# The last 64 keys' products with v as four 64 by 64 tiles, issued in front of the next scores

## The chip, the cores and the metric

One Trainium2 chip, one of its cores. The metric is the device time of one execution in microseconds (us), as the median of several runs. The engines are TensorE (PE, matmuls; PEld is its weight load), VectorE (DVE), ScalarE (ACT), GpSimd (POOL) and SyncE (SP, which issues DMAs).

## What is computed

```python
# q, k, v: (8 batches, 8 heads, 576 positions, 64), float32
scores = 1 / sqrt(64) * q @ k.T
scores = where(scores >= max(scores, -1) - tau, scores, -1e9)
attn   = exp(scores - max(scores, -1));  attn /= sum(attn, -1) + 1e-9
x      = heads side by side of (attn @ v)          # (8, 576, 512)
xn     = (x - mean) / sqrt(var + 1e-6) * g_ln      # over the 512 features
out    = x + max(xn @ w_ch1, 0) @ w_ch2            # 512 -> 2048 -> 512
```

## The kernel before, in words

**Slots.** A batch is worked off in nine slots (`SLOTS`), 72 in all (`NS`). Slots 0 to 3 take two heads each and their first 256 queries (`QH`), slot 4 (`s == HP`) takes the last 32 queries of each half for all heads, and slots 5 to 8 take the second 256 queries. In each slot the loop from L949 calls, in program order: the scores of this slot (L957), maxima, thresholds and exponentials (`exponentials`, L396), masks and sums (`weights`, L417), and the turning of the weights so that keys lie on partitions. Each engine works off its own instructions strictly in the order in which this loop issues them.

**Quarters.** A slot is cut into four quarters. `at_quarter(n, i, fn)` (L886) books a call for quarter `i` of slot `n`, and `run(n, i)` (L889) makes the booked calls; quarter -1 comes between the scores and the exponentials. Between them `second_part` (L900) puts in matmuls of the feed-forward part of an earlier group (a group is half a batch, 288 positions), as many as the planner's account of steps allows. So PE's queue is a chain of feed-forward matmuls (line L101, by the helper `product`, which splits a product into two column tiles of 64) into which scores and products with v are set.

**Scores.** `scores` (L373) multiplies the turned q by the turned k. The contraction is over 64 numbers, so it uses row tiles of 64: the two heads go to two PSUM tiles `sc[0]` and `sc[1]` of three banks each, in pieces of 384, 192, 320 and 256 columns (L390). In slot 4 these are four 64 by 64 tiles (`q_last`). The pieces lie at columns 128 to 1279 of each tile.

**Turned weights.** In batch 0, `turn_weights` (L452) turns the weights on PE by multiplying by a diagonal matrix, into tiles `tp` (512 keys, L461) and `tr` (the last 64 keys, L478), and ACT copies them to `em` and `er`. In later batches, `turn_blocks` (L493) turns 32 by 32 blocks on DVE, writes them to DRAM (`scr`), and `fetch` (L515), at quarter 0 of the next slot, reads them back: `em`, 512 keys as four chunks of 128, and `er`, the last 64 keys, on partitions 0 to 63 of one of two buffers `rests`, whose other 64 partitions are zero.

**Products with v.** `values_of` (L532) is booked for quarter 3 of the next slot (quarter 1 for the first five slots, `b == 0 and s <= HP`). For each of the two heads it multiplies the four chunks of v (`vt`) and then the last 64 keys (`vr`, from `v_rest`, partitions 64 to 127 zero) by 256 columns of weights (L550), all as 128 by 64 tiles. The result `pv` lies behind the scores in `sc[0]`, at columns 1280 to 1535 (`pv_behind`, L362), in the bank that holds the last scores too. In the first five slots it lies in a tile of its own. In slot 4 there are four pairs of heads of 64 columns each. After it ACT copies `pv` to `x` (L567, or L558 in slot 4), and POOL adds it to the sum over features (`add_feature`, L576).

**After the products.** `group_ready` (L925) books the mean of a group (`mean_of`, L585, a matmul that needs the sum), the centring (L599, DVE) and the feed-forward part two slots or so after its last product. `mean_of` puts itself off while the segments of the second feed-forward product hold both banks of PSUM. The relu of the first feed-forward product is ACT's (L729). Its PSUM tiles take turns between two banks.

**Loads.** `load_v` (L125) loads `vt` and `vr` for a pair of heads; POOL clears `rests` and `v_rest` once at the start (L151). SP issues these, the writes and reads of `scr`, the loads of q and k, and the stores. POOL scales q (L338) before DVE turns it (L345).

Of the kernel before, what the change touches and what calls it, by code (L numbers as in the profile page):

```python
# [8 lines left out]
F32 = mybir.dt.float32  # L9
# [9 lines left out]
def kernel(  # L19
# [31 lines left out]
    nc = tc.nc  # L51
    B, H, S, D = q.shape
# [41 lines left out]
    loaded, values_in, turned = {}, {}, {}  # L94
# [30 lines left out]
    def load_v(u):  # L125
        b, hp = units[u]
        vt = ins.tile([128, 2, J, D], F32, tag="v", name="v_in")
        vr = v_rest[hp]
        both = v[b, 2 * hp : 2 * hp + 2]
        if b:  # L130
            nc.sync.dma_start(
                out=vt.rearrange("p h c d -> p h (c d)"),
                in_=both[:, : J * 128].rearrange("h (p c) d -> p h (c d)", c=J),
            )
        for h in range(0 if b else 2):
            nc.sync.dma_start(
                out=vt[:, h], in_=both[h, : J * 128].rearrange("(c p) d -> p c d", p=128)
            )
# [257 lines left out]
    def exponentials(n):  # L396


        neg = small.tile([128, 4], F32, tag="neg", name="neg")
        thr = small.tile([128, 4], F32, tag="thr", name="thr")  # L400
        es = e_room[(n + 1) % 2 if n < SLOTS else 0]
        for h in range(2):
            i = slice(2 * h, 2 * h + 2)
            nc.vector.tensor_reduce(  # L404
                out=neg[:, i], in_=pairs[h],
                axis=AXL.X, op=ALU.max, negate=True,
            )
            nc.gpsimd.tensor_scalar(  # L408
                out=thr[:, i], in0=neg[:, i], scalar1=-1.0, scalar2=low_sb,
                op0=ALU.mult, op1=ALU.add,  # L410
            )
        for i in range(4):
            if i == 2:
                yield es, thr
            nc.scalar.activation(es[:, i], blocks[i], func=AF.Exp, bias=neg[:, i : i + 1])  # L415
# [31 lines left out]


    def turned_tiles(s):
        return att.tile([128, 4, J, 128], F32, tag="em", bufs=1, name="em"), rests[s % 2]  # L450

    def turn_weights(s, es, diags):  # L452


        em, er = turned_tiles(s)
        for i in range(4):
            if i:
                yield
            tp = ps_ff.tile([128, J, 128], F32, tag="ff", name="tp")
            for c in range(J):  # L460
                product(  # L461
                    tp[:, c], lhsT=es[:, i, c * 128 : (c + 1) * 128], rhs=diags[i],
                    start=True, stop=True,
                )
# [12 lines left out]
        for i in range(4):  # L477
            nc.tensor.matmul(  # L478
                tr[:, i], lhsT=es[:, i, J * 128 :], rhs=diags[i], start=True, stop=True
            )  # L480
        if s == HP:
            nc.scalar.copy(
                er[:64].rearrange("p a (u x) -> p u a x", u=HP),
                tr.rearrange("p u (a x) -> p u a x", a=4),
            )
        else:
            nc.scalar.copy(
                er[:64].rearrange("p a (h x) -> p h a x", h=2),
                tr.rearrange("p (h j) (a x) -> p h (j a) x", h=2, a=2),
            )  # L490
        yield em, er

# [34 lines left out]
    def x_of(g):  # L527
        if g not in groups:
            groups[g] = ffn.tile([128, NK, TOK], F32, tag="x", bufs=3, name="x")
        return groups[g]  # L530

    def values_of(b, s, turned_weights):  # L532

        em, er = turned_weights
        pv = pv_behind
        if b == 0 and s <= HP:
            pv = ps_ff.tile([128, QH], F32, tag="ff", name="pv")
        if s == HP:
            outs = [(hp, pv[:, hp * 64 : hp * 64 + 64]) for hp in range(HP)]
            pick = lambda t, hp, h: t[  # L540
                :, hp % 2 * 2 : hp % 2 * 2 + 2, (2 * h + hp // 2) * 32 : (2 * h + hp // 2) * 32 + 32
            ]
        else:
            outs = [(s if s < HP else s - HP - 1, pv)]
            pick = lambda t, hp, h: t[:, :, 64 * h : 64 * h + 64]
        for hp, dst in outs:
            vt, vr = values_in[b * HP + hp]
            for c in range(J + 1):
                for h in range(2):
                    nc.tensor.matmul(  # L550
                        dst[64 * h : 64 * h + 64],
                        lhsT=vt[:, h, c, :] if c < J else vr[:, h, :],
                        rhs=pick(em[:, :, c] if c < J else er, hp, h),
                        start=(c == 0), stop=(c == J),
                    )
        if s == HP:
            for t in range(2):
                nc.scalar.copy(  # L558
                    x_of(2 * b + t)[:, :, QH:],
                    pv.rearrange("p (u t x) -> p t u x", u=HP, t=2)[:, t],  # L560
                )
                for c in range(1, NK):
                    add_feature(2 * b + t, c, slice(QH, TOK))
        else:
            g = 2 * b + (s > HP)
            hp = outs[0][0]
            nc.scalar.copy(x_of(g)[:, hp, :QH], pv)  # L567
            if hp:
                add_feature(g, hp, slice(0, QH))
# [379 lines left out]
    for n in range(NS):  # L949
        b, s = divmod(n, SLOTS)  # L950
        ticks = (1, 3, 4)[: 2 + n // 3] if n < 6 else range(1, 7)

        def tick(i):
            if i in ticks:
                conversion.tick()

        scores(b, s)  # L957
        run(n, -1)
        rest = exponentials(n)
        es, thr = next(rest)  # L960
# [61 lines left out]
        drip({nc.vector: 2, nc.gpsimd: 0})  # L1022
    while later_calls or queue or aside or stores or drops:
        n += 1
        for i in range(QUARTERS):
# [35 lines left out]
```

## Time and profile before

| | |
|---|---|
| median of 3 runs | 1397.54 us (1396.71 to 1398.15) |
| the profiled execution | 1397.5 us, of which the span is 1395.7 us |
| PE busy | 1337.3 us, 96% of the span |
| DVE, POOL, ACT busy | 931.2, 609.7, 460.4 us |
| scores (L390), products with v (L550), busy | 150.6 and 130.8 us and smaller groups |
| granted clock of PE, mean | 0.993 |

The profile records one execution. The span is the time from its first instruction to its last; the rest of the execution's time lies around it. A float32 matmul leaves two records. A matmul's record is longer than the time for which it keeps the next one from starting, since they are pipelined; so what a group of matmuls costs is read from the starts of the groups behind it, not from the mean length of a record.

### The profile page before, as it was taken

The numbers are of one execution on the slowest core, as the hardware profiler recorded it, in microseconds if no ns is written. First come the engines' busy times: TensorE is split into PE (matmuls) and PEld (weight loads), VectorE is DVE, ScalarE is ACT, GpSimd is POOL, SyncE is SP. The second block draws the span as 40 slices with busy tenths as digits, with TensorE's granted clock in tenths as the row PEclk, the third lists the DMA queues.
The fourth block names the chain that finished last, engine by engine and source line by source line (L and its number), as shares of the span: only waits on it lengthen the run. The fifth ranks groups of instructions, "written<-read, shape, count | busy, mean of one in ns | idle before, by whom it ended". The sixth has DMA issues, their size and how long they took to land.

```text
span 1395.7 us, 35606 instructions
## 1 busy us (share of the span) xinstructions
PE 1337.3 (96%) x15048; PEld 986.9 (71%) x15048; DVE 931.2 (67%) x1638; ACT 460.4 (33%) x923; POOL 609.7 (44%) x809
## 2 busy tenths in 40 slices
PE   4888999999999999999999999999999999999996
PEld 3665665867768596877869586776858677685966
DVE  5998967676776767657776767657775767766211
ACT  3877613232332323232232323323232323323120
POOL 2444444544433454343444455353444444334413
PEclk8999999999999999999999999999999999999998
DMA  9722355447744476446754477445764476443211
GB/s 231 175 77 70 95 145 153 154 146 187 196 133 159 136 191 180 142 137 185 192 160 146 150 196 188 138 148 151 187 180 143 134 183 184 127 161 129 63 18 18
DMA packets 316383, 205.48 MB, mean 147 GB/s; under 512 B 242368, under 2 KB 273856, under 8 KB 308160
## 3 DMA queue, kind: packets, MB, share of 16 engines
q1 hardware_dynamic: 311456, 202.62, 50.8%
q8 instruction: 118, 1.93, 0.6%
q10 hardware_dynamic: 4736, 0.59, 0.4%
q14 instruction: 41, 0.34, 0.1%
q0 software_dynamic: 32, 0.00, 0.0%
HBM read 119.41 MB, written 83.76 MB: 146 GB/s over the span
## 4 chain that ended last, share of the span: by engine, by line
PE 89%; DVE 5%; ACT 2%; issue 1%; POOL 0%; POOLq 0%; DVEq 0%; ACTq 0%
PE p L101 36%; PE seg L101 30%; PE sc L550 10%; PE sc L390 10%; DVE e L422 1%; PE tp L101 1%; DVE neg L404 1%; PE var L101 0%; PE mean L101 0%; DVE w L269 0%; ACT e L415 0%; PE tr L478 0%; ACT part L812 0%; DVE hidden L296 0%; DVE w L296 0%
## 5 line engine op out<-in xcount | busy, mean ns | idle before, releaser
L101 PE MATMUL p<-xc,w 128*64 128x288 f32 x4096 | 518.1, 408 | 13.0 <-ACT hidden L729 5.5
L101 PEld LDWEIGHTS p<-xc,w 128*64 128x64 f32 x4096 | 288.9, 137 | 224.6 <-ACT hidden L729 16.0
L404 DVE TENSOR_REDUCE neg<-sc 128x2 f32<-128x1152 f32 x144 | 188.8, 1352 | 271.1 <-PE sc L390 271.0
L415 ACT ACTIVATE e<-sc,neg 128x576 f32<-128x576 f32 x288 | 196.8, 744 | 247.7 <-DVE neg L404 247.7
L438 POOL TENSOR_SCALAR e<-e,den 128x576 f32<-128x576 f32 x252 | 194.1, 783 | 134.5 <-DVE den L427 134.3
L101 PE MATMUL seg<-hidden,w 128*64 128x144 f32 x3840 | 248.0, 287 | 0.0
L101 PEld LDWEIGHTS seg<-hidden,w 128*64 128x64 f32 x3840 | 235.1, 137 | 11.6 <-issue 7.7
L422 DVE SCALAR_TENSOR_TENSOR e<-sc,thr,e 128x576 f32<-128x576 f32 x288 | 222.0, 810 | 13.9 <-ACT e L415 13.2
L729 ACT ACTIVATE hidden<-p 128x288 f32<-128x288 f32 x256 | 105.9, 414 | 241.0 <-PE p L101 239.2
L408 POOL TENSOR_SCALAR thr<-neg,low_sb 128x2 f32<-128x2 f32 x144 | 42.5, 295 | 306.1 <-DVE neg L404 302.1
L390 PE MATMUL sc<-kT,qT 64*128 64x384 f32 (+3 forms) x1024 | 150.6, 425 | 20.1 <-DVE qT L350 10.1
L504 DVE STREAM_TRANSPOSE et<-e 128x1152 f32<-128x1152 f32 x112 | 153.1, 1374 | 14.8 <-POOL e L438 14.0
L390 PEld LDWEIGHTS sc<-kT,qT 64*128 64x128 f32 x1024 | 94.3, 191 | 69.9 <-issue 18.2
L550 PE MATMUL sc<-em,v_in 128*64 128x256 f32 (+1 forms) x1408 | 130.8, 329 | 0.0
L101 PE MATMUL seg<-hidden,stage 128*64 128x144 f32 x1920 | 123.1, 286 | 0.0
L101 PEld LDWEIGHTS seg<-hidden,stage 128*64 128x64 f32 x1920 | 117.9, 137 | 3.5 <-issue 2.3
L550 PEld LDWEIGHTS sc<-em,v_in 128*64 128x64 f32 x1408 | 86.4, 137 | 32.2
L797 POOL TENSOR_TENSOR hidden<-hidden 128x576 f32<-128x576 f32 x60 | 84.4, 1426 | 27.3 <-ACT hidden L729 19.0
L576 POOL TENSOR_TENSOR sum<-sum,x 128x256 f32<-128x256 f32 (+1 forms) x64 | 32.6, 509 | 113.2 <-ACT x L567 110.7
L797 DVE TENSOR_TENSOR hidden<-hidden 128x576 f32<-128x576 f32 x60 | 49.1, 853 | 47.8 <-PE seg L101 38.1
L567 ACT COPY x<-sc 128x256 f32<-128x256 f32 x60 | 22.3, 372 | 164.7 <-PE sc L550 115.3
L812 ACT COPY part<-seg 128x288 f32<-128x288 f32 x75 | 30.1, 401 | 131.2 <-PE seg L101 109.6
(151 smaller groups left out, 1186.6 us busy)
## 6 DMA issues: line engine op xcount, KB each, us to landing
scr<-et SPq DMA_DIRECT2D x63, 1152.0 KB, 4.9
em<-scr SPq DMA_DIRECT2D x63, 1024.0 KB, 5.9
out_dram<-ot SPq DMA_DIRECT2D x256, 36.0 KB, 4.9
q_in<-in_q_dram SPq DMA_DIRECT2D x124, 72.0 KB, 2.7
k_in<-in_k_dram SPq DMA_DIRECT2D x120, 72.0 KB, 3.0
rest<-scr SPq DMA_DIRECT2D x63, 128.0 KB, 6.0
v_in<-in_v_dram SPq DMA_DIRECT2D x28, 256.0 KB, 5.2
w<-in_moe_w_ch_dram SPq DMA_DIRECT2D x10, 512.0 KB, 6.2
```

The lines of the kernel that those rows point to most:

```text
L101: nc.tensor.matmul(out[r], lhsT=lhsT[:, r], rhs=rhs, **flags)
L390: nc.tensor.matmul(sc[h][64 * i : 64 * i + 64 if s == HP else 128, at : at + n], lhsT=ql[r] if s == HP else qT[r, half, j * 128 : (j + 1) ...
L404: nc.vector.tensor_reduce(out=neg[:, i], in_=pairs[h], axis=AXL.X, op=ALU.max, negate=True,)
L408: nc.gpsimd.tensor_scalar(out=thr[:, i], in0=neg[:, i], scalar1=-1.0, scalar2=low_sb, op0=ALU.mult, op1=ALU.add,)
L415: nc.scalar.activation(es[:, i], blocks[i], func=AF.Exp, bias=neg[:, i : i + 1])
L422: nc.vector.scalar_tensor_tensor(out=es[:, i], in0=blocks[i], scalar=thr[:, i : i + 1], in1=es[:, i], op0=ALU.is_ge, op1=ALU.mult, accum_o ...
L438: nc.gpsimd.tensor_scalar(out=es[:, i], in0=es[:, i], scalar1=den[:, i : i + 1], scalar2=1.0, op0=ALU.mult, op1=ALU.mult,)
L504: nc.vector.transpose(et[:, :, 64 * h : 64 * h + 64].rearrange("p n (j c) -> p j n c", j=2), es[:, 2 * h : 2 * h + 2].rearrange("p j (n c) ...
L550: nc.tensor.matmul(dst[64 * h : 64 * h + 64], lhsT=vt[:, h, c, :] if c < J else vr[:, h, :], rhs=pick(em[:, :, c] if c < J else er, hp, h) ...
L576: nc.gpsimd.tensor_tensor(out=sums[g][:, cols], in0=x[:, 0, cols] if c == 1 else sums[g][:, cols], in1=x[:, c, cols], op=ALU.add,)
L729: nc.scalar.activation(hidden[:, d], p1, func=AF.Relu)
L797: eng.tensor_tensor(out=out[at], in0=in0[at], in1=in1[at], op=op)
```

## The change

The products of the 512 keys are cut in two halves of 128 columns (`j`), of which one goes to the columns behind `sc[0]` and one to those behind `sc[1]`. They stay at quarter 3. The last 64 keys are laid out twice as high: `er` has the queries of half 0 on partitions 0 to 63 and those of half 1 on 64 to 127, in one buffer, and `v_rest` holds v's last 64 rows on both halves of the partitions, loaded twice. Their products are four tiles of 64 rows by 64 columns, two heads by two halves of the queries, issued at a new point, quarter -3, just in front of the scores of the slot after next. ACT's copy of half 1 comes at quarter -2, just behind these scores; its copy of half 0 comes at a point "copy" in `exponentials`, behind the maxima and thresholds and in front of the first exponential. POOL's sums come at quarter 0 of that slot. For the first five slots all of it stays in place, with a rest on 128 rows (the other half is zero). The turned leftover `tr` of batch 0 is written to two column tiles instead of one.

```diff
-    rests = [consts.tile([128, 4, 128], F32, name=f"rest{i}") for i in range(2)]
-    v_rest = [consts.tile([128, 2, D], F32, name=f"v_rest{i}") for i in range(HP)]
+    er_sb = consts.tile([128, 2, 128], F32, name="er")
+    v_rest = [consts.tile([128, 2, 2, D], F32, name=f"v_rest{i}") for i in range(HP)]
...
-        nc.sync.dma_start(out=vr[:64], in_=both[:, J * 128 :].rearrange("h p d -> p h d"))
+        for j in range(2):
+            nc.sync.dma_start(
+                out=vr[64 * j : 64 * j + 64, j], in_=both[:, J * 128 :].rearrange("h p d -> p h d")
+            )
...
-    for t in rests + v_rest:
+    for t in v_rest:
         nc.gpsimd.memset(t, 0.0)
...
-    pv_behind = sc[0][:, FREE + 2 * S : FREE + 2 * S + QH]
+    pv_behind = [t[:, FREE + 2 * S : FREE + 2 * S + 128] for t in sc]
...
+        run(n, "copy")
         for i in range(4):
             if i == 2:
                 yield es, thr
...
-        tr = ps_ff.tile([64, 4, 128], F32, tag="ff", name="tr")
+        tr = ps_ff.tile([128, 2, 128], F32, tag="ff", name="tr")
         for i in range(4):
-            nc.tensor.matmul(
-                tr[:, i], lhsT=es[:, i, J * 128 :], rhs=diags[i], start=True, stop=True
-            )
+            rest = es[:, i, J * 128 :]
+            if s == HP:
+                to = tr.rearrange("p a (b x) -> p (a b) x", b=2)[:, i]
+                for half in range(2):
+                    at = slice(64 * half, 64 * half + 64)
+                    nc.tensor.matmul(to[at], lhsT=rest, rhs=diags[i][:, at], start=True, stop=True)
+            else:
+                h, j = divmod(i, 2)
+                nc.tensor.matmul(
+                    tr[64 * j : 64 * j + 64, h], lhsT=rest, rhs=diags[i], start=True, stop=True
+                )
...
-        nc.sync.dma_start(out=er[:64], in_=scr[:, J * 128 :].rearrange("a p x -> p a x"))
+        for j in range(2):
+            nc.sync.dma_start(
+                out=er[64 * j : 64 * j + 64],
+                in_=scr[2 * j : 2 * j + 2, J * 128 :].rearrange("a p x -> p a x"),
+            )
...
+        for c in range(J):
+            for (hp, j, dst, pick), first in zip(outs, firsts):
+                vt, _ = values_in[b * HP + hp]
                 for h in range(2):
                     nc.tensor.matmul(
-                        dst[64 * h : 64 * h + 64],
-                        lhsT=vt[:, h, c, :] if c < J else vr[:, h, :],
-                        rhs=pick(em[:, :, c] if c < J else er, hp, h),
-                        start=(c == 0), stop=(c == J),
+                        dst[64 * h : 64 * h + 64], lhsT=vt[:, h, c, :],
+                        rhs=pick(em[:, 2 * j : 2 * j + 2, c], h), start=c == 0 and first, stop=False,
                     )
+        def rest():
+            for (hp, j, dst, pick), last in zip(outs, lasts):
+                _, vr = values_in[b * HP + hp]
+                rows = slice(0, 128) if at_once else slice(64 * j, 64 * j + 64)
+                for h in range(2):
+                    nc.tensor.matmul(
+                        dst[64 * h : 64 * h + 64], lhsT=vr[rows, j, h],
+                        rhs=pick(er[rows], h), start=False, stop=last,
+                    )
...
+        if at_once:
+            rest()
+            copy(0)
+            copy(1)
+            add()
         else:
+            n = b * SLOTS + s + 2
+            at_quarter(n, -3, rest)
+            at_quarter(n, -2, copy, 1)
+            at_quarter(n, "copy", copy, 0)
+            at_quarter(n, 0, add)
...
+        run(n, -3)
         scores(b, s)
+        run(n, -2)
         run(n, -1)
```

More of the change, by code (lines that the diff above doesn't have):

```diff
@@ L449, in turned_tiles @@
     def turned_tiles(s):
-        return att.tile([128, 4, J, 128], F32, tag="em", bufs=1, name="em"), rests[s % 2]
+        return att.tile([128, 4, J, 128], F32, tag="em", bufs=1, name="em"), er_sb
     def turn_weights(s, es, diags):
@@ L475, in turn_weights @@
                 )
-        tr = ps_ff.tile([64, 4, 128], F32, tag="ff", name="tr")
+        tr = ps_ff.tile([128, 2, 128], F32, tag="ff", name="tr")
         for i in range(4):
-            nc.tensor.matmul(
-                tr[:, i], lhsT=es[:, i, J * 128 :], rhs=diags[i], start=True, stop=True
-            )
+            rest = es[:, i, J * 128 :]
[9 more added lines that the diff above has]
+                )
         if s == HP:
             nc.scalar.copy(
-                er[:64].rearrange("p a (u x) -> p u a x", u=HP),
-                tr.rearrange("p u (a x) -> p u a x", a=4),
+                er.rearrange("p a (u x) -> p u a x", u=HP),
+                tr.rearrange("p v (w a x) -> p (v w) a x", w=2, a=2),
             )
@@ L487, in turn_weights @@
             nc.scalar.copy(
-                er[:64].rearrange("p a (h x) -> p h a x", h=2),
-                tr.rearrange("p (h j) (a x) -> p h (j a) x", h=2, a=2),
+                er.rearrange("p a (h x) -> p h a x", h=2),
+                tr.rearrange("p h (a x) -> p h a x", a=2),
             )
@@ L534, in values_of @@
         em, er = turned_weights
+        at_once = b == 0 and s <= HP
         pv = pv_behind
-        if b == 0 and s <= HP:
-            pv = ps_ff.tile([128, QH], F32, tag="ff", name="pv")
+        if at_once:
+            both = ps_ff.tile([128, 2, 128], F32, tag="ff", name="pv")
+            pv = [both[:, j] for j in range(2)]
         if s == HP:
-            outs = [(hp, pv[:, hp * 64 : hp * 64 + 64]) for hp in range(HP)]
-            pick = lambda t, hp, h: t[
-                :, hp % 2 * 2 : hp % 2 * 2 + 2, (2 * h + hp // 2) * 32 : (2 * h + hp // 2) * 32 + 32
-            ]
-        else:
-            outs = [(s if s < HP else s - HP - 1, pv)]
-            pick = lambda t, hp, h: t[:, :, 64 * h : 64 * h + 64]
@@ L546, in values_of @@
-        for hp, dst in outs:
-            vt, vr = values_in[b * HP + hp]
-            for c in range(J + 1):
+            outs = [
+                (hp, hp % 2, pv[hp % 2][:, hp // 2 * 64 : hp // 2 * 64 + 64],
+                 lambda t, h, hp=hp: t[:, :, (2 * h + hp // 2) * 32 : (2 * h + hp // 2) * 32 + 32])
+                for hp in range(HP)
+            ]
+        else:
+            outs = [
+                (s % (HP + 1), j, pv[j], lambda t, h: t[:, :, 64 * h : 64 * h + 64])
+                for j in range(2)
+            ]
@@ L549, in values_of @@
+        banks = [0 if at_once else j for _, j, _, _ in outs]
+        firsts = [banks.index(bank) == i for i, bank in enumerate(banks)]
+        lasts = [bank not in banks[i + 1 :] for i, bank in enumerate(banks)]
+        for c in range(J):
+            for (hp, j, dst, pick), first in zip(outs, firsts):
+                vt, _ = values_in[b * HP + hp]
                 for h in range(2):
                     nc.tensor.matmul(
-                        dst[64 * h : 64 * h + 64],
-                        lhsT=vt[:, h, c, :] if c < J else vr[:, h, :],
@@ L553, in values_of @@
-                        rhs=pick(em[:, :, c] if c < J else er, hp, h),
-                        start=(c == 0), stop=(c == J),
-                    )
-        if s == HP:
-            for t in range(2):
+                        dst[64 * h : 64 * h + 64], lhsT=vt[:, h, c, :],
+                        rhs=pick(em[:, 2 * j : 2 * j + 2, c], h), start=c == 0 and first, stop=False,
+                    )
+        def rest():
[7 more added lines that the diff above has]
+                    )
@@ L558, in values_of, with copy @@
+        def copy(j):
+            if s == HP:
+                for t in range(2):
+                    nc.scalar.copy(
+                        x_of(2 * b + t)[:, :, QH:].rearrange("p (a j) x -> p j a x", j=2)[:, j],
+                        pv[j].rearrange("p (a t x) -> p t a x", a=2, t=2)[:, t],
+                    )
+            else:
                 nc.scalar.copy(
-                    x_of(2 * b + t)[:, :, QH:],
-                    pv.rearrange("p (u t x) -> p t u x", u=HP, t=2)[:, t],
-                )
@@ L562, in values_of, with add @@
-                for c in range(1, NK):
-                    add_feature(2 * b + t, c, slice(QH, TOK))
-        else:
[L565 to L569, printed above, removed]
+                    x_of(2 * b + (s > HP))[:, s % (HP + 1), 128 * j : 128 * j + 128], pv[j]
+                )
+        def add():
+            if s == HP:
+                for t in range(2):
+                    for c in range(1, NK):
+                        add_feature(2 * b + t, c, slice(QH, TOK))
+            elif s % (HP + 1):
+                add_feature(2 * b + (s > HP), s % (HP + 1), slice(0, QH))
@@ L571, in add_feature @@
+        if at_once:
+            rest()
+            copy(0)
+            copy(1)
+            add()
+        else:
+            n = b * SLOTS + s + 2
[3 more added lines that the diff above has]
+            at_quarter(n, 0, add)
     def add_feature(g, c, cols):
@@ L1024 @@
         n += 1
+        for i in (-3, -2, -1, "copy"):
+            run(n, i)
         for i in range(QUARTERS):
```

## The prediction, made before the change was run

> **What bounds the kernel now.** I read the page's busy times and its chain first.
>
> ```profile
> PE 1337.3 (96%) x15048; PEld 986.9 (71%) x15048; DVE 931.2 (67%) x1638; ACT 460.4 (33%) x923; POOL 609.7 (44%) x809
> ...
> PE 89%; DVE 5%; ACT 2%; issue 1%; POOL 0%; POOLq 0%; DVEq 0%; ACTq 0%
> ```
>
> TensorE (PE) holds the end: 89% of the chain. The table of stretches agrees: from 240 to 1310 us PE is busy 1065.6 of 1070. So there, what PE no longer streams is gained in full, and what it newly waits for is lost in full. Before 240 us, DVE and ACT take turns on the chain, and each item has to be looked up there.
>
> Next the PE timeline of one slot in the middle. Columns: start, length, operation, records. Two matmuls side by side leave four records, so two records are one pass of a pair. Lengths overlap, so I use differences of starts.
>
> ```profile
> 613.16 1.90 PE L550 MATMUL sc<-em,v_in 128*64 128x256 f32 x16
> 614.89 0.60 PE L550 MATMUL sc<-rest,v_rest 128*64 128x256 f32 x4
> 615.32 2.60 PE L101 MATMUL p<-xc,w 128*64 128x288 f32 x20
> 617.85 2.21 PE L390 MATMUL sc<-kT,qT 64*128 64x384 f32 x16
> 619.99 6.04 PE L101 MATMUL p<-xc,w 128*64 128x288 f32 x48
> 625.86 0.66 PE L101 MATMUL var<-hidden,avg_sb 128*64 128x288 f32 x4
> ```
>
> The last 64 keys (rest) cost 615.32 - 614.89 = 0.43 us: two passes of 256 columns, 0.216 each, 0.84 ns a column. A pass of 288 columns takes 0.243. The ten passes from 615.32 should end at 617.75, but the scores start at 617.85: 0.10 late. The scores stream 2 x 1152 columns, 1.94 us, and hold PE 2.14: 0.20 more. The 24 passes after them take 5.87, not 5.82: 0.05 more. So a visit to the 64-row, 128-column shape costs 0.35 us beyond its columns. The same reading for the scores of the last queries, which run as 64 by 64 tiles:
>
> ```profile
> 243.20 1.62 PE L101 MATMUL p<-xc,w 128*64 128x288 f32 x12
> 244.75 2.17 PE L390 MATMUL sc<-kT,q_last 64*64 64x384 f32 x32
> 246.85 2.16 PE L101 MATMUL p<-xc,w 128*64 128x288 f32 x16
> 248.84 0.91 PE L101 MATMUL seg<-hidden,w 128*64 128x144 f32 x12
> ```
>
> 0.10 before, 2.10 - 1.94 = 0.16 inside, 0.05 after: 0.31. And 32 records in the time of 16 say that four 64 by 64 tiles do run together, at the column rate of two.
>
> [...]
>
> **Part by part, steady state.** 67 slots' products use the deferred path (63 of batches 1 to 7, and four of batch 0).
> - Rest: four tiles of 128 columns together, 2 passes x 0.109 = 0.22, for 0.43: -0.21.
> - em products: 8 passes of 256 become 16 of 128. Transposes of 128 columns (tp) take 3.58 us for 32 passes, entry included, so a pass costs 0.109 to 0.112 and loads don't bind. 16 x 0.109 = 1.75 for 1.73: +0.02 (0.00 to 0.07).
> - One more change of shape per slot: [...] +0.16. No row shows 64 by 64 going to 64 by 128. [...] Dearer than any seen is possible; I allow +0.06.
>
> Of the 67, 51 are followed by wide scores: -0.03 each, -1.5 us. Seven stand before the 64 by 64 scores, so no change is added: -0.19 each, -1.3. Seven are the last-query products: their 40 passes with em take 2.33 us (273.56 to 275.89), 0.058 each; rest goes from 8 passes to 4, -0.23 + 0.16 = -0.07 each, -0.5. The last two have no scores behind them and pay a whole visit: +0.12 each, +0.2. Sum -3.1 us.
>
> **Batch 0.** Here the weights are turned on PE, and the leftover (tr) goes from one column tile to two.
>
> ```profile
> 122.28 3.75 PE L101 MATMUL tp<-diag,e 128*64 128x128 f32 x64
> 125.86 1.07 PE L478 MATMUL tr<-diag,e 128*64 128x128 f32 x8
> 126.72 2.15 PE L101 MATMUL p<-xc,w 128*64 128x288 f32 x16
> ```
>
> Eight records in 0.86 us, one tile at a time; paired, 0.43. Four of nine (97, 126, 148, 180 us) lie on PE's part of the chain: -1.7. The one at 32 us lies on the chain with its ACT copy (0.58 for 512 elements per partition; 256 take 0.37): -0.6. The other four are covered by DVE, whose pieces fill the chain from 36 to 89 us: nothing. SyncE issues each rest of v twice (0.7 to 1.9 us each at the start) ahead of the weight fetches. First use of a weight chunk is at 18.2 us, with issue at 10.9 and 5.5 to land: nothing taken, up to +1.5. In the first five slots the rest stays on 128 rows, 4 passes of 128 for 2 of 256: nothing. POOL's first memsets differ by less than 1 us and end near 2.3 us; its next work waits for q until 8.8: nothing.
>
> **What moves.** The copies go to the head of the next slot.
>
> ```profile
> 620.16 2.62 DVE L404 TENSOR_REDUCE neg<-sc 128x2 f32<-128x1152 f32 x2 [7.55 <-PE sc L390]
> 621.61 1.37 ACT L415 ACTIVATE e<-sc,neg 128x576 f32<-128x576 f32 x2 [3.23 <-DVE neg L404]
> 622.87 0.41 ACT L729 ACTIVATE hidden<-p 128x288 f32<-128x288 f32 x1
> ```
>
> Copy 1 waits for the scores and runs under the first maximum (1.35 us). The second maximum waits for it: hidden. Copy 0 waits for the first maximum and delays both exponentials and the relu behind them. A copy of 256 takes 0.37, of 288 0.40: 128 about 0.26, less overlap, so 0.2 to 0.3 late. PE needs that relu's bank at 619.99 + 0.05 + 16 x 0.243 = 623.93; it is free at 623.28: 0.65 in hand. The last-query slot copies in four pieces, perhaps 0.4 late: still covered. DVE's masks come 0.3 later; the next scores are 8 us behind them.
>
> POOL's sums move behind the thresholds. For even groups six adds (1.74 us at 596.7) then end about 4.9 us after the scores; the mean on PE comes 5.7 after: covered by 0.8. Where the head also scales q, the sum stands ahead of that. This costs only where the chain goes through it, once:
>
> ```profile
> 195.27 0.06 POOL thr L408
> 195.34 0.18 issue
> 195.52 0.75 POOL q_in L338
> 196.28 0.02 issue
> 196.30 0.04 DVE qT L345
> ```
>
> One add of 0.74 goes in front of q_in: +0.74 at the next start of PE (201.73), which now waits 1.86 there for DVE. The early mean at 194.85 will wait some 1.4 inside that same time. At 232.96 the exponentials are on the chain: copy 0 adds 0.2. Sum +0.9. On SyncE one more DMA per slot (leftover in two halves) sits behind em's at the slot's head, needed a slot later; with one buffer instead of two it waits for the rest products, which stand before the scores, while its issue comes 1.2 us after their start (635.90 to 634.67): nothing.
>
> **Sum.** -3.1 - 2.3 + 0.9 = -4.5 us. The profiled execution took 1397.5 us (span 1395.7 and 1.8 around it), like the median of 1397.54: 1393.0.
>
> **Rivals.** (1) [...] 0.21 less on 58 slots, -12 us more, 1381. [...] (2) The change is dearer than any seen, or four tiles that accumulate lose a little: 0.06 to 0.09 over 58 slots takes back 3.5 to 5 us: 1396.5 to 1398, no difference. (3) Slower: relus at the slots' heads. Two heads in each of 14 groups have 0.65 us in hand. If copy 0 (its wait, its time, its handover) comes to 0.95 us instead of 0.3, PE stands 0.3 at each of 28 heads, +8: 1401. It decides from 0.65 on. For it: the copy is in front of everything ACT does then. Against it: the waits show no such stall today,
>
> ```profile
> PE p L101 <- ACT hidden L729: 5.5, 3, 2.8
> ```
>
> three times in all, at the start, and no copy of this size nears 0.65.
>
> **Numbers.** The forecast case has 0.64, spread 1389.5 to 1396.5 by the switch's bounds; 0.10 of it lies within 0.2% (2.8 us, about what a measurement of this kernel can tell from no change). Rival 1: 0.11, faster. Rival 2: 0.14, of it 0.02 slower. Rival 3: 0.11, of it 0.01 within. Faster 0.65, same 0.23, slower 0.12. From 1387 to 1399 leaves out most of rivals 1 and 3.
>
> **What would show it.** In the timeline after: rest as 8 records in about 0.22 plus 0.05, a first score 0.22 late, em in 1.75, p to rest 0.10. tr in 0.43. No new row "PE p <- ACT hidden" in the middle; PE's mean at 195 waiting for POOL. Wrong, if rest to scores shows no gap (rival 1) or over 0.3 (rival 2), or if p waits for ACT in every group (rival 3).

## The result, and the profile after

The changed kernel takes 1399.23 us, median of 4 runs (1396.44 to 1400.06), against 1397.57 for the kernel before in the same comparison: a ratio of 1.0009 with a 95% interval from 0.9991 to 1.0026. No difference can be told. The forecast was 1393.0, faster; the result lies 6.2 above it, at the upper edge of the range that was given (1387 to 1399). The profiled execution took 1399.81 us, span 1398.0.

The page's busy times and its chain, for the changed kernel:

```profile
PE 1332.8 (95%) x16336; PEld 1011.1 (72%) x16336; DVE 928.2 (66%) x1638; ACT 464.2 (33%) x1003; POOL 607.1 (43%) x807
...
PE 83%; DVE 7%; ACT 2%; DMA 2%; issue 2%; POOL 1%; SPq 1%; POOLq 0%; DVEq 0%; ACTq 0%
```

PE is 4.5 us less busy, and yet the end is no earlier: PE's share of the chain fell from 89% to 83%, DVE's rose from 5% to 7%, and POOL now has a share. From 240 to 1310 us PE is busy 1061.9 of 1070, where it was 1065.6. So the work became shorter and PE waits more. First the work: PE's timeline of the middle slot that the prediction read, in the changed kernel (start, length, operation, records).

```profile
614.81 1.92 PE L574 MATMUL sc<-em,v_in 128*64 128x128 f32 x32
616.56 2.60 PE L101 MATMUL p<-xc,w 128*64 128x288 f32 x20
619.08 0.45 PE L584 MATMUL sc<-er,v_rest 64*64 64x128 f32 x8
619.46 2.21 PE L393 MATMUL sc<-kT,qT 64*128 64x384 f32 x16
621.60 6.04 PE L101 MATMUL p<-xc,w 128*64 128x288 f32 x48
```

The products with em take 616.56 - 614.81 = 1.75, as worked out. Ten passes of p end at 616.56 + 2.43 = 618.99 and the rest starts at 619.08: 0.09 for the change of shape. From the rest to the scores 0.38; if the columns take 0.22 of it, as worked out from passes of 128, 0.16 is the second change. The scores hold PE 2.14, as before. In front of the 64 by 64 scores the same rest takes less:

```profile
246.02 0.45 PE L584 MATMUL sc<-er,v_rest 64*64 64x128 f32 x8
246.29 2.12 PE L393 MATMUL sc<-kT,q_last 64*64 64x384 f32 x32
```

0.27 instead of 0.38, for no change of shape lies between. All this is as forecast. Now the waits of PE, from the table of waits (engine, line, tile, releaser: us in total, times, longest):

```profile
PE p L101 <- ACT hidden L779: 5.5, 3, 2.7
...
PE seg L101 <- DVE hidden L847: 3.8, 6, 0.6
...
PE mean L101 <- POOL sum L626: 1.2, 1, 1.2
```

The first line, rival 3's, is what it was before (5.5, three times). The second is new: six times 0.63, once in each of batches 2 to 7, between the scores of their slots 1 and 2. The third is new too, and foreseen.

How one of the six comes about is seen in the timelines of the same place (a bracket gives the idle time ahead of an instruction and what ended it). The kernel before:

```profile
833.67 8.23 PE L101 MATMUL seg<-hidden,w 128*64 128x144 f32 x128
...
835.05 0.27 POOL L408 TENSOR_SCALAR thr<-neg,low_sb 128x2 f32<-128x2 f32 x1 [0.99 <-DVE neg L404]
835.30 0.74 POOL L338 TENSOR_SCALAR q_in<-q_in,scl_sb 128x576 f32<-128x576 f32 x1
...
836.00 0.81 POOL L816 TENSOR_TENSOR y<-y 128x288 f32<-128x288 f32 x1
836.07 0.77 DVE L345 STREAM_TRANSPOSE qT<-q_in 128x256 f32<-128x256 f32 x2 [0.45 <-POOL q_in L338]
...
836.89 1.38 POOL L816 TENSOR_TENSOR y<-y,part 128x288 f32<-128x288 f32 x1
836.90 1.99 DVE L797 TENSOR_TENSOR hidden<-hidden 128x576 f32<-128x576 f32 x2
```

PE's segments stand in one group, without a wait in the table. The changed kernel:

```profile
835.32 4.09 PE L101 MATMUL seg<-hidden,w 128*64 128x144 f32 x64
...
836.63 0.27 POOL L411 TENSOR_SCALAR thr<-neg,low_sb 128x2 f32<-128x2 f32 x1 [0.99 <-DVE neg L407]
...
836.86 0.73 POOL L626 TENSOR_TENSOR sum<-sum,x 128x256 f32<-128x256 f32 x1
...
837.58 0.75 POOL L341 TENSOR_SCALAR q_in<-q_in,scl_sb 128x576 f32<-128x576 f32 x1
...
838.36 0.77 DVE L348 STREAM_TRANSPOSE qT<-q_in 128x256 f32<-128x256 f32 x2 [1.15 <-POOL q_in L341]
...
839.18 2.00 DVE L847 TENSOR_TENSOR hidden<-hidden 128x576 f32<-128x576 f32 x2
...
840.04 2.18 PE L101 MATMUL seg<-hidden,w 128*64 128x144 f32 x32 [0.63 <-DVE hidden L847]
```

The sum stands between the second threshold and q_in. DVE's turn of q waits for it 0.70 longer, and what is queued behind that turn on DVE has nothing to do with q: the operand difference for PE's next segments (L847). Before, it started 836.90 - 833.67 = 3.23 us behind the segments; here it starts 839.18 - 835.32 = 3.86 behind, and PE waits 0.63. Even before it came without slack: in a run further down, where it starts 3.16 behind, the 128 records that take 8.23 here take 8.16.

### The profile page after: what moved, and what is told of

The parts are those of the page before. It is cut to its first block, busy times and chain, and to the rows that moved or that the text cites. A ratio compares the mean times of both kernels' runs of the same rounds, so it can differ in the third digit from the quotient of the medians.

```text
span 1398.0 us, 38357 instructions
## 1 busy us (share of the span) xinstructions
PE 1332.8 (95%) x16336; PEld 1011.1 (72%) x16336; DVE 928.2 (66%) x1638; ACT 464.2 (33%) x1003; POOL 607.1 (43%) x807
## 4 chain that ended last, share of the span: by engine, by line
PE 83%; DVE 7%; ACT 2%; DMA 2%; issue 2%; POOL 1%; SPq 1%; POOLq 0%; DVEq 0%; ACTq 0%
PE p L101 34%; PE seg L101 27%; PE sc L393 10%; PE sc L574 8%; PE sc L584 2%; DVE e L426 2%; DVE neg L407 1%; DMA v_in<-in_v_dram 1%; SPq L116 1%; PE tp L101 1%; DMA et<-in_moe_w_ch_dram 1%; POOL q_in L341 1%; PE var L101 0%; PE mean L101 0%; POOL sum L626 0%
## 5 line engine op out<-in xcount | busy, mean ns | idle before, releaser
L574 PE MATMUL sc<-em,v_in 128*64 128x128 f32 (+1 forms) x2368 | 129.5, 263 | 0.0
L574 PEld LDWEIGHTS sc<-em,v_in 128*64 128x64 f32 x2368 | 122.9, 137 | 7.8
L597 ACT COPY x<-sc 128x128 f32<-128x128 f32 x120 | 31.8, 266 | 260.7 <-PE sc L393 193.5
L847 POOL TENSOR_TENSOR hidden<-hidden 128x576 f32<-128x576 f32 x60 | 84.8, 1429 | 47.8 <-ACT hidden L779 38.2
L847 DVE TENSOR_TENSOR hidden<-hidden 128x576 f32<-128x576 f32 x60 | 49.2, 854 | 49.1 <-PE seg L101 39.1
L101 PE MATMUL seg<-hidden,e 128*64 128x144 f32 x960 | 65.3, 286 | 0.0
```

The source lines that it names most:

```text
L101: nc.tensor.matmul(out[r], lhsT=lhsT[:, r], rhs=rhs, **flags)
L574: nc.tensor.matmul(dst[64 * h : 64 * h + 64], lhsT=vt[:, h, c, :], rhs=pick(em[:, 2 * j : 2 * j + 2, c], h), start=c == 0 and first, stop= ...
L597: nc.scalar.copy(x_of(2 * b + (s > HP))[:, s % (HP + 1), 128 * j : 128 * j + 128], pv[j])
L847: eng.tensor_tensor(out=out[at], in0=in0[at], in1=in1[at], op=op)
```

## The experiments

Most alter one thing, in the changed kernel or in the one before; two put two edits together. To see where in the run a difference arises, I list when PE starts the scores of a slot, as the offset to the kernel before in the profiled executions (us; "end" is PE's last matmul). "Sum at head" is the kernel before with the sums moved; "behind q" and "behind adds" are the changed kernel with the sums later, "and mean" the latter with a later mean; "v upper" is the kernel before with the added loads.

```
slot   changed  sum at head  behind q  behind adds  and mean  v upper
  2     -1.78      -1.26       -0.78      -0.97      -1.25     -0.22
  4      1.60      -1.33       -1.39       2.63      -0.02     -0.21
  7      0.78       0.36       -0.57       1.86      -1.08     -0.18
  9      0.74       0.38       -0.63       1.83      -2.25      0.38
 11      1.70       1.77        0.80       1.89      -3.64      0.39
 18      1.28       1.71        0.37       1.48      -1.41      0.40
 71      2.12       5.93       -0.03      -1.87      -4.52      0.43
end      2.35       5.93        0.20      -1.63      -4.28      0.43
```

Up to slot 7 single executions differ by up to 4 us (in slot 4 by -1.39 to 2.63 among four kernels whose program is the same there). So the place of a loss is read from slot 7 on, and the start from medians only. In part this is the granted clock of PE. It was 0.50 from 18.5 to 28.5 us in the kernel before, and from 49.5 to 52.5 and from 77 to 80 us in the changed one. Between slots 6 and 7, ten passes that take 2.65 us in both of these, at a clock of 1.00, take 4.22 in "behind q"; the offset there rises by 1.6.

**The sums alone.** The kernel before, with nothing altered but the place of POOL's sums: at the head of a later slot, as in the changed kernel.

```diff
...
-            if hp:
-                add_feature(g, hp, slice(0, QH))
+            add = lambda: hp and add_feature(g, hp, slice(0, QH))
+        if b == 0 and s <= HP:
+            add()
+        else:
+            at_quarter(b * SLOTS + s + 2, 0, add)
```

> The kernel before with only POOL's sums moved, to quarter 0 of the next slot, in front of the scaling of q. Theory A (this move alone makes the stalls): six or seven waits of PE seg for DVE hidden of about 0.6 us, and 0.4 and 0.6 at slots 9 and 10: +4.5 to +5, 1402 to 1402.6. Rival B (it takes the late exponentials as well): fewer waits, 1398 to 1399.5.

Measured: 1402.70 us against 1397.58, ratio 1.0038 (1.0024 to 1.0052). Its table of waits:

```profile
PE seg L101 <- DVE hidden L802: 4.2, 6, 0.7
PE mean L101 <- POOL sum L581: 1.3, 1, 1.3
```

Six times 0.70, and 1.39 between slots 9 and 11 in the offsets. This one move costs 5.1 us and makes both waits, without any of the changes on PE. Turned round: the change without it should beat the kernel before by some 3 to 4 us.

**The sums behind q.** The changed kernel, with the sum behind the scaling of q instead of ahead of it.

```diff
-            at_quarter(n, 0, add)
+            at_quarter(n, "sum", add)
...
                 load_qk(u + 1)
+        run(n, "sum")
         if n < SLOTS + HP:
...
```

> The changed kernel with POOL's sums over features issued behind the scaling of q instead of in front of it. Theory A (the sum in front of q's scaling makes DVE late; once per batch PE then waits 0.63 us for the operand difference that DVE has behind its transposes, and slots 9 and 10 lose about 0.4 and 0.6): the six waits of PE seg for DVE hidden vanish, -3.8 us, and about -0.4 to -0.9 at slots 9 and 10 (the early mean still waits for the sum): 1394 to 1396. Rival B (the stall comes from the copies on ACT or from DVE's second maximum waiting for a copy): the six waits stay, 1399.

Measured: 1398.69 us (1397.12 to 1402.28) against 1397.28, ratio 1.0013 (1.0007 to 1.0020). That can't be told apart from the changed kernel, and is not what I expected. By the offsets, slots 18 to 71 fall by 0.40, where the changed kernel's rise by 0.84. The waits say why:

```profile
PE seg L101 <- DVE hidden L847: 2.5, 6, 0.4
PE mean L101 <- POOL sum L626: 1.9, 1, 1.9
```

The stall has shrunk to 0.41 and is not gone. The same place in this kernel's timeline:

```profile
836.05 0.73 POOL L626 TENSOR_TENSOR sum<-sum,x 128x256 f32<-128x256 f32 x1
836.12 0.77 DVE L348 STREAM_TRANSPOSE qT<-q_in 128x256 f32<-128x256 f32 x2 [0.44 <-POOL q_in L341]
836.74 0.80 POOL L866 TENSOR_TENSOR y<-y 128x288 f32<-128x288 f32 x1
...
836.94 2.48 DVE L847 TENSOR_TENSOR hidden<-hidden 128x576 f32<-128x576 f32 x2
...
838.30 4.14 PE L101 MATMUL seg<-hidden,w 128*64 128x144 f32 x64 [0.41 <-DVE hidden L847]
```

DVE turns q in time again (0.44 of idle). But the sum has pushed POOL's add of y to 836.74, just ahead of DVE's difference. Of the difference's two instructions the first takes 1.21 instead of 0.72 and ends at 838.15, 0.61 after the add has ended (836.74 + 0.80 = 837.54). The add starts 0.20 ahead, and of the 0.60 us that the two stand side by side, DVE loses 0.49. In the kernel before this add ends at 836.81, ahead of the difference at 836.90. A second add starts there 0.01 ahead of the difference (836.89), and it is that add which is longer (1.38; another of its kind takes 0.79 at 599.35). What decides which of the two takes longer is not shown.

**The sums behind the adds.** So the sum goes later still, ahead of POOL's scaling of the weights, where it stands idle for 2.4 us. In the last-query slot and slot 10, where a mean needs the sum at once, it stays at the head.

```diff
-            at_quarter(n, 0, add)
+            at_quarter(n, 0 if s == HP or n == 10 else "sum", add)
...
         tick(2)
+        run(n, "sum")
         blocks_go = by_blocks(b * HP)
...
```

> The changed kernel with POOL's sums put still later in the slot: behind the scaling of q and behind the adds of y, just ahead of POOL's scaling of the weights, where POOL stands idle for 2.4 us. The two kinds of slot whose mean on TensorE needs the sum at once (the last-query slot and slot 10) keep it at the head. Theory A: the trace of the run with the sum directly behind q shows q on time (0.44 us of idle ahead of qT, as before the change), but now the sum delays POOL's adds of y by 0.7, so that they run beside the whole of DVE's operand difference, which takes 2.48 instead of 1.99, and PE still waits 0.4 six times. With the adds back in their place the six waits and the 0.37 at slot 9 go: 3.8 + 0.4 less than the changed kernel, so 1394.7 to 1395.5, and no row of seg waiting for DVE over 0.1. Theory B (the wait comes from DVE's own lateness after the copies, whatever POOL does): 0.4 stays six times and the time is 1398 to 1399.

Measured: 1394.70 us (1393.03 to 1399.93) against 1397.95, ratio 0.9978 (0.9970 to 0.9987). As theory A, and faster than both kernels. Its timeline:

```profile
833.43 8.16 PE L101 MATMUL seg<-hidden,w 128*64 128x144 f32 x128
...
835.70 0.80 POOL L866 TENSOR_TENSOR y<-y 128x288 f32<-128x288 f32 x1
...
836.59 1.99 DVE L847 TENSOR_TENSOR hidden<-hidden 128x576 f32<-128x576 f32 x2
...
837.93 1.24 POOL L626 TENSOR_TENSOR sum<-sum,x 128x256 f32<-128x256 f32 x1
```

The first add is ahead of the difference again, the difference takes 1.99, and no row of seg waiting for it is left. The offsets go from 1.48 in slot 18 to -1.87 in slot 71, by -3.35, where the changed kernel's go up by 0.84: 4.2 between them, six times 0.70. Of each 0.70, 0.63 are the changed kernel's stall and 0.07 what the kernel before lost there too.

**And the mean later.** On top of that, the mean of the second group and the steps behind it come a quarter of a slot later, so that its sum can be late too.

```diff
-            at_quarter(n, 0 if s == HP or n == 10 else "sum", add)
+            at_quarter(n, 0 if s == HP else "sum", add)
...
-            return (24, 42)[g]
+            return (24, 43)[g]
```

> As the run with the sums behind the adds of y, and the second group's mean and the steps behind it one quarter of a slot later, so that its sum can be late too. Theory A: the wait of the mean for the sum (1.2 us in slot 10, which moved the next scores by 0.58) goes as well: 0.5 to 0.6 below that run. Theory B: the group that starts a quarter later has to be made up in the following slots, or DVE is as late there for another reason: within 0.3 of that run or above it.

Measured: 1392.74 us (1392.31 to 1393.47), ratio 0.9965 (0.9952 to 0.9978), the fastest kernel here. The mean no longer waits for the sum, but for something else:

```profile
PE mean L101 <- DVE o L687: 1.6, 1, 1.6
```

By the offsets it gains 3.2 us from slot 7 to the end, no more than the kernel ahead of it (3.5): what it is early by in slots 9 to 11 is given back by slot 18, as theory B said. The rest of its advantage in the median would lie in the start. The two intervals overlap, so whether the later mean itself is worth anything stays open.

**The added loads.** In the first of two runs, the kernel before loads each rest of v twice to the same place.

```diff
-        nc.sync.dma_start(out=vr[:64], in_=both[:, J * 128 :].rearrange("h p d -> p h d"))
+        for _ in range(2):
+            nc.sync.dma_start(out=vr[:64], in_=both[:, J * 128 :].rearrange("h p d -> p h d"))
```

> The kernel before with each load of v's last 64 rows issued twice, to the same place: the start's extra DMAs alone. Theory A (SP issues q and k later[...]): the third slot's scores start 0.5 to 2 us later and the end moves by as much, 1398 to 1399.5. Rival B (in the kernel before DVE has other work until q and k are there): within 0.4 us of before, 1397.6.

Measured: 1408.18 us, ratio 1.0080 (1.0066 to 1.0094): 10.6 more, all of it by slot 7. This tests the wrong thing. The second load writes where the first writes, and in SP's queue the issues take 3.94 and 7.24 us for two, where one took 0.73 and 1.85 before. I read that as the second load waiting for the first.

```profile
10.09 3.94 SPq L140 DMA_DIRECT2D v_rest<-in_v_dram  x2
...
17.20 7.24 SPq L140 DMA_DIRECT2D v_rest<-in_v_dram  x2
```

In the second run the copy goes to the unused upper half of the tile (`for t in (vr[:64], vr[64:])`).

> The kernel before with each rest of v loaded a second time, now into the unused upper half of its own tile, whose products meet weights of zero; so neither load waits for the other. This is the changed kernel's number of loads by SyncE, and nothing else of it. Theory A (the added loads cost the start what the changed kernel lost there, the upper end given in the prediction): 1.0 to 1.5 us over the kernel before, all of it ahead of slot 7. Theory B (the first 100 us hide them, and the offsets of single profiles there, from -2.2 to +1.6, are the spread of the start): within 0.4 of the kernel before. The earlier run with both loads into the same place gave +10.6, which A and B both put down to the second waiting for the first.

Measured: 1397.91 us against 1397.95, ratio 1.0006 (0.9998 to 1.0014). The medians are equal, and the offsets ahead of slot 7, where theory A puts the loss, are -0.2. That speaks for B; the interval, -0.3 to 2.0 us, doesn't exclude A. The other side of the same question is the changed kernel with the second half loaded behind the next q and k:

```diff
...
+        half(0)
+        halves.append(lambda: half(1))
...
                 load_qk(u + 1)
+        run_all(halves)
```

> The changed kernel with the second load of v's last 64 rows issued behind the next loads of q and k instead of in front of the weight fetches and of q and k. Theory A (the start's gain is lost because SP issues the extra loads in front of q and k, so DVE waits some 3 us for k at the third slot): that wait falls below 1.5 us and the fourth slot starts 1 to 2.5 us earlier, 1397 to 1398. Rival B (k is late for bandwidth, or the weights' conversion on DVE bounds the start anyway): the slots after the sixth start within 0.3 us of where they did, 1399.

Measured: 1399.03 us (1396.33 to 1401.49), ratio 1.0012 (1.0004 to 1.0020): no gain. The edit did less than theory A asked for, since DVE's wait for k at the third slot fell only to 2.58. I had suspected the loads for a wait of DVE for k in the changed kernel's profile, which was not there before:

```profile
42.90 0.78 DVE L344 STREAM_TRANSPOSE kT<-k_in 128x576 f32<-128x576 f32 x1 [3.37 <-DMA k_in<-in_k_dram]
```

What it costs by slot 7 lies within the scatter of that stretch. Both edits together, the loads and the sums behind q:

> Both edits together. If the two losses are apart, their gains add: 1392.5 to 1395, that is 3 to 5 us below the kernel before, from -3.1 us in the steady slots and what the start keeps. If the start is bound by DVE's conversion, 1394.5 to 1396.

Measured: 1399.29 us (1395.22 to 1400.75), ratio 1.0011 (1.0004 to 1.0017), no different from the sums behind q alone; so the loads show no cost here either.

**The turning in batch 0.** First from the other side: the kernel before with half of tr left out (`range(4)` to `range(2)`, and half of its copy).

> The kernel before with half of the leftover's turning left out in batch 0 (two of four products and half of the copy): half of the last 64 keys is missing there. Theory A (behind the turning, PE waits for the bank of the last turned tile, which ACT's copy frees only 0.6 us later, so that a shorter turning buys nothing): slots 5 to 8 keep their spacing within 0.1 us, and a wait of p for ACT em of about 0.2 appears three or four times. Rival B: 0.43 less in each of slots 6, 7 and 8, 1.3 us in all.

Measured: 1395.42 us in one run. By the offsets it is 2.63 early in slot 6, but 1.61 in slot 7 and 1.58 in slots 8 and 9: with tr as short as in the change, slots 7 and 8 gain nothing. (Slot 6 loses 1.0, in the stretch where executions scatter.) Both that kernel and the changed one show a wait that takes the place of the work; the changed kernel's row:

```profile
PE p L101 <- ACT em L476: 0.7, 3, 0.2
```

p takes a PSUM bank over from the last tp, and ACT's copy of that tp (0.59 us) isn't done. In the changed kernel's timeline:

```profile
126.64 0.64 PE L490 MATMUL tr<-diag,e 128*64 128x128 f32 x8
126.86 0.59 ACT L476 COPY em<-tp 128x512 f32<-128x512 f32 x1 [0.29 <-PE tp L101]
...
127.49 2.16 PE L101 MATMUL p<-xc,w 128*64 128x288 f32 x16 [0.21 <-ACT em L476]
```

tr to p takes 0.85, as it took 0.86 with the long tr. To see whether the bank is the cause, half of this last copy was left out in the changed kernel.

```diff
+                part = slice(0, 2)
+                if i == 3 and s > HP:
+                    nc.gpsimd.memset(em[:, 3, :, 64:], 0.0)
+                    part = slice(0, 1)
```

> The changed kernel with half of the last of four copies of turned weights left out in four slots of batch 0 (POOL writes zeros there instead), so that ACT frees the PSUM bank about 0.22 us earlier. Leaves out part of the weights of keys before the last 64 in these slots. Theory A (the shorter turning of the last 64 keys gains nothing because the first layer's next product waits 0.2 to 0.25 for that bank): this wait goes, and slots 6 to 9 take 0.2 less each: 0.6 to 0.9 below the changed kernel, 1398.3 to 1398.7, and no row of p waiting for the copy of turned weights. Theory B (the chain of those slots runs through ACT's exponentials or the relus, which come no earlier or lose it again): no change in the spacing of those slots, 1399.0 to 1399.5.

Measured: 1399.40 us (1396.03 to 1403.42), ratio 1.0012 (1.0006 to 1.0019), as theory B. But the table no longer has the wait for the copy, and slots 6 and 7 are 0.21 and 0.23 shorter than in the changed kernel (offsets 0.33, 0.17, -0.07 in slots 6, 7, 8 against 0.73, 0.78, 0.77). Tr to p takes 0.64 there instead of 0.85, and p still starts just behind the copy's end (126.67 after 126.62), so no run shows the 0.43. In slot 9 the gain is given back: tp waits there for DVE 1.8 us, where the changed kernel waits 0.8.

```profile
PE tp L101 <- DVE o L691: 1.8, 1, 1.8
```

So each theory holds in part: the wait for the copy takes the gain first, and behind it DVE's work of slot 9 does.

**The shape of the rest.** The changed kernel with the rest on 128 rows, half of them zeros, at the same place (`rows = slice(0, 128)`): one change of shape fewer and twice the passes.

> The changed kernel with the last 64 keys' products on all 128 rows, the other half of v's rows being zero: four tiles of 64 columns, two at a time, in the same place, without the 64 by 64 shape. Theory A (the four tiles save 0.21 us of streaming and pay 0.16 for one more change of shape): rest takes 0.44 instead of 0.38 with its change, +0.06 on 51 slots and about +0.2 on the 7 slots in front of 64 by 64 scores, +0.07 on 7: +4 to +5 us, 1403 to 1404. Rival B (the place in front of the scores and not the tiles gave the steady slots their 0.03): no difference, 1399.

Measured: 1403.28 us, ratio 1.0044 (1.0030 to 1.0058), 4.1 over the changed kernel, as theory A. By the offsets to the changed kernel a slot with wide scores takes 0.06 more and one with the last queries' scores 0.17.

**Its place.** The changed kernel with the rest right behind em's products (`rest()` for `at_quarter(n, -3, rest)`).

> The changed kernel with the 64 by 64 products directly behind those of the 512 keys, at quarter 3, and not in front of the scores. Theory A (what counts is the number of changes of shape: here a whole visit of its own, 0.31, instead of 0.16): +0.15 us on some 51 slots, +0.3 on the 7 in front of 64 by 64 scores, +0.15 on 7: +10 to +11 us, 1409 to 1410. Rival B (the place doesn't matter, a change of shape costs only where weights are wide): +0 to +3.

Measured: 1410.65 us, ratio 1.0089 (1.0075 to 1.0103), 11.4 over the changed kernel, a little above theory A's range. By the offsets a slot with wide scores takes 0.15 more and one with the last queries' scores 0.26, as theory A. The rest has a change of shape on both sides here, and the scores have theirs besides; beside the scores one of them is shared.

## Where the prediction held and where it failed

**Right: the work on PE.** In the kernel with the sums behind the adds, a slot with wide scores gains 0.03 by the offsets, as forecast; one in front of the 64 by 64 scores gains 0.14 and 0.05 more in the slot behind it (forecast 0.19); the last-query products gain 0.07 to 0.08 (0.07). Slots 18 to 71 give -3.35. The -3.1 was for all 67 slots, some -2.8 of it for these; 0.4 of the rest are the six places at which the kernel before had lost 0.07. The added change of shape, which no row of before showed, was taken as 0.16, an estimate of mine. In the timeline the rest takes 0.09 + 0.38, for 0.43 and the 0.10 in front of the scores before; with em's 0.02 that is 0.04 a slot, 0.03 by the offsets. How the change divides is not shown: the records of the weight loads, 0.132 us long for the rest and 0.187 for the wide scores, don't tell how much of it is a load. The lower end of the prediction's spread, 1389.5, does not follow from a change that costs nothing: 58 times 0.16 would be 9.3.

**Right: the odds against the rivals.** Rival 1 (no gap between two shapes of 64 rows; its odds were my estimate) would have the scores follow the rest after 0.22; they follow after 0.38. Rival 2 needed a change dearer by 0.06 to 0.09; it is not. Rival 3 needed relus late in every group; "PE p <- ACT hidden" stands at three times, as before. None of the three signs that I named for a wrong forecast appeared; it failed for a reason that I had not named. That the time still lies at the edge of the range is luck: that end was drawn for rival 2, which didn't occur.

**Failed, the step that decided: "Where the head also scales q, the sum stands ahead of that. This costs only where the chain goes through it, once".** I followed the sum to q_in and to qT, and looked for where the chain of waits of before ran through them. That chain shows what was last before the change. Behind qT on DVE stands the operand difference, which the chain doesn't show: it came as PE needed it, at most 0.07 late. A delay of 0.73 on a queue without slack is paid at once: PE waits 0.63 in each of batches 2 to 7, 3.8 us over the kernel before, forecast as nothing. The run with the sums alone moved makes these waits, and the one with the sums behind the adds is free of them. The one place that was priced, at 195 us, was given 0.74 and took 0.59 (offset 1.11 to 1.70); the mean there waits 1.2 for the sum, forecast 1.4.

**Failed: batch 0, -1.7 for four shorter tr.** The prediction asked whether tr lies on PE's part of the chain. It does. It did not ask what p, the next on PE, waits for besides: the bank that ACT's copy holds. A copy that ends 0.22 earlier gives 0.21 and 0.23 in slots 6 and 7, so half of the 0.43 hangs on it there; for the other half and for the other two places the cause is not shown. Of the places that were put at nothing as covered by DVE, those between the scores of slots 4 and 6 gain 0.3 and 0.6, in every kernel here with the shorter tr, the kernel before with half of tr among them. The -0.6 at 32 us can't be seen in the scatter of the start.

**Failed in size only: +0.2 for copy 0 at 232.96.** From slot 12 to 13 the offset falls by 0.12 (1.66 to 1.54), and in the later batches, at the same kind of slot, by 0.14 to 0.15. So copy 0 cost some 0.03.

**Unsettled: "nothing taken" for SP's added loads.** The medians agree with nothing, the interval allows up to 2.0 us.

**The account.** From slot 7 to the end the forecast's terms are -3.5: the steady slots -3.1, three shorter tr -1.3, POOL's sum and copy 0 +0.9. The profiled execution shows +1.6 there (0.78 to 2.35). The six stalls add 3.8 and the three tr 1.3, and the sum at 195 us and copy 0 took 0.3 less: +1.3, so 0.3 stay unexplained. Ahead of slot 7 the forecast was -1.0 and this execution has +0.8, in a stretch where executions differ by more than that; what is real of it stays open.

## What to carry to other kernels

When an instruction moves ahead of another on an in-order engine, follow not only the tile that becomes late but everything queued behind its reader, and ask of each how long before its use it was ready: a chain of waits shows what was last, and a thing that was ready just in time isn't in it. Here it was 0.07 us late, too little for a row. The place of a small step counts more than its length: the same add of 0.73 us cost PE 3.8 us ahead of q_in, 2.5 behind it, and nothing behind the adds of y. And where work on the busiest engine gets shorter, look up what else the next instruction waits for, the one that frees its PSUM bank among it.

## What the runs showed of the hardware

- Four tiles of 64 rows by 64 columns ran side by side while accumulating in two banks: 8 records of 128 columns, with the step to the next products of that shape, took 0.27 us. With the step to 64 by 128 they took 0.38, so this change of the columns alone cost 0.11 more.
- Beside one another, DVE's difference and POOL's adds took longer. With POOL's add of y 0.20 us ahead, the first instruction of the difference took 1.21 us instead of 0.72 (the sums behind q); with an add of y 0.01 ahead, that add took 1.38 instead of 0.79 (the kernel before); a sum beside the end of the difference took 1.24 instead of 0.73 (the sums behind the adds).
- Loading the same 64 rows twice cost 10.6 us when both loads had one destination, and nothing that could be told when they had two (1397.91 us against 1397.95). With one destination two issues took 3.94 and 7.24 us in SP's queue, where one took 0.73 and 1.85; whether the program or the queue asks for that is not shown.
- The granted clock of PE fell to 0.50 for 3 to 10 us at a time in the first 100 us of both profiled executions, of the kernel before and of the changed one. Where it fell differed: from 20 to 40 us its mean was 0.79 in the kernel before and 1.00 in the changed one, from 40 to 60 us 1.00 and 0.91.
